# Loading the first output's weights: into the decoding's free places and into x's place after the last sums, instead of into x's place piece by piece

## The chip, the cores and the metric

One program on one core of a Trainium2 chip. The metric is the device time of one execution in microseconds (us); lower is better. Times of the kernel before come from three timed executions and from one profiled execution.

## The reference

```python
kv  = einsum('bhsd,bhse->bhde', k, v)            # 4 batches, 8 heads, 576 tokens, 64 wide
out = einsum('bhsd,bhde->bhse', q, kv)
x   = out / sqrt(mean(out*out) + 1e-6) * g_norm  # as 2304 tokens x 512
y   = ((x @ w_a) * (x @ w_b)) @ w_out            # 512 -> 1536 -> 512, the "first output" is y
h   = y @ w_in                                   # 512 -> 1024
s   = h * softmax(h); ln = layernorm(s) * g_ln
res = ln @ w_out2                                # 1024 -> 512
```

Everything is float32; the weights arrive as 64-bit floats.

## The kernel before, in words

**Arithmetic.** A float32 operand is kept as two parts, hi and lo, and each product is three matmuls on TensorE: hi*hi, lo*hi and hi*lo (lines 1035 to 1037 for the sums, line 1390 for the first output). The 64-bit weights are decoded on ScalarE (ACT), VectorE (DVE) and GpSimd (POOL); weights that are used later are written to HBM in hi and lo (line 588) and read back when their place is free.

**Stages.** First attention makes x. Then come the two products x @ w_a and x @ w_b, called the sums here. The d_ff dimension has 12 slices f of 128 and they are done in pairs fp. The last pairs use a scheme of seven block products (P1 to P7) over three token groups t, of 768 tokens each; a block product is done for w_a and then for w_b, six matmuls each. The products a*b go to HBM (`gm`, line 1057). Then y is computed (line 1390): 5 blocks j of tokens (384, 384, 512, 512, 512), within a block the 12 slices f, for each f four output slices d of 128, three matmuls each. For each (j, f) a tile `gi` is read from `gm` (line 1336), split into `gh` and `gl` (ACT line 1363, DVE line 1364), and multiplied with `wo[f]`, the hi and lo of w_out's slice f (512 KB). Then follows the second layer.

**Where x and wo lie.** x takes 73,728 bytes of each partition from offset XB on, in three pieces of tokens: 0 to 383, 384 to 1919 and 1920 to 2303 (line 281). A piece holds four planes of hi and then four planes of lo, one plane for 128 of the 512 channels. In the middle piece a plane is 6144 bytes. The weights of the first output reuse x's place (lines 309 to 316): wo[0] to wo[2] take the first piece, wo[3] to wo[8] the first 4096 bytes (tokens 384 to 1407) of six planes of the middle piece, wo[9] part of the last piece, and wo[10] and wo[11], in two halves of 256 KB each, the last 2048 bytes (tokens 1408 to 1919) of the first four planes of the middle piece.

**What sets the order.** The program's order on every engine is written out by a planner (`Order`) that keeps its own estimate of the time. All loads are issued by SyncE (SP), in order, on one queue. `c_loads` (line 1327) issues the loads of `gi` and of `wo`. A `wo[f]` is loaded when it is in HBM, when the planner's DMA backlog is under 3 us, and when in the last pair the token groups whose x lies in its place are done: t = 0 for f 0 to 2, t = 0 and 1 for f 3 to 8, all three for f 9 to 11. `c_item` (line 1371) holds the matmuls of one (j, f); its `ready` waits for the split `gi` and for `wo[f]`. Up to the last block products, items of the first output are put between them where `b_items` has fewer than three left. The semaphores between engines are set by the framework from the tiles that instructions read and write.

**The end of the sums in the last pair.** Token group 2 (tokens 1536 to 2303) runs last, in the order P1, P5, P2, P6, P3, P7, P4. P2 multiplies the raw x: for tokens 1536 to 1919, planes 2 and 3 of hi and lo in the middle piece. P5, P6 and P7 read sums kept elsewhere (`th`, `tl`), P3 and P4 the last piece. When no block product is left, the decoding of w_in opens (line 1767), and SP loads `raw` tiles of 512 KB for it (line 404).

**Free places.** The decoding uses WS (8192 bytes: two `f` tiles and the `ws` tiles) and STG (two staging tiles of 4096 bytes) until the last of w_out is in HBM. After that STG and WS are next written as the second half of w_in's sums (`bo`, line 323).

Of the kernel before, what the change touches and what calls it, by code (L numbers as in the profile page):

```python
# [9 lines left out]
F32 = mybir.dt.float32  # L10
F32R = mybir.dt.float32r
# [6 lines left out]
P = 128  # L18
# [5 lines left out]
NF1 = DF1 // P  # L24
# [13 lines left out]
CH = 512  # L38
# [167 lines left out]
def attention_moe_moe_kernel(ctx: ExitStack, tc, kv_in, kv_tail, q_in, g_norm, w1, w_in, w_out2, g_ln, out):  # L206
# [3 lines left out]
    nc = tc.nc  # L210
    INF = float("inf")
    M = Map(nc)
# [5 lines left out]
    od = Order()  # L218
# [9 lines left out]
    def ps_ready():  # L228
        return min(place_time(i) for i in range(4))
# [4 lines left out]
    def ps_tile(want=None):  # L234
        i = min(range(4), key=lambda i: (place_time(i) > od.now, want is not None and (i in wide) != want, place_time(i)))
        assert place_time(i) < INF
        bank[2 * i] = bank[2 * i + 1] = INF
        return i, PS[:, 2 * i:2 * i + 2]

    def ps_done(i):  # L240
        def done(t):
            bank[2 * i] = bank[2 * i + 1] = t

        return (None, 0, done)
# [61 lines left out]
    s_t = [M(f"s{i}", [P, 2, TB], F32, (M.R2 + 36864, M.R2 + 39936, M.AB + 4096)[i]) for i in range(3)]  # L306


    WO_AT = [4096 * f for f in range(3)] + [12288 + 6144 * k for k in range(6)] + [69632, (16384, 22528), (28672, 34816)]
    wo = []  # L310
    for f, at in enumerate(WO_AT):
        if isinstance(at, tuple):
            wo.append([M(f"wo{f}{n}", [P, CH], F32R, M.XB + a) for n, a in enumerate(at)])
        else:
            w = M(f"wo{f}", [P, 2, CH], F32R, M.XB + at)
            wo.append([w[:, 0], w[:, 1], w])
    gi_t = [M(f"gi{i}", [P, CH], F32, (M.T0 + 12288 if i < 3 else M.R2 + 6144) + 2048 * i) for i in range(6)]
    gs_t = [[M(f"g{x}{i}", [P, CH], F32R, M.R2 + 4096 * i + 2048 * n) for n, x in enumerate("hl")] for i in range(3)]
    ya = [M("ya0", [P, NP, HALVES[0]], F32, M.XB + 49152), M("ya1", [P, NP, HALVES[1]], F32, M.R2 + 18432)]
# [16 lines left out]
    def half(tok):  # L336
        return (0, tok) if tok < HALVES[0] else (1, tok - HALVES[0])
# [6 lines left out]
    for fp in range(PLAIN // 2, NF1 // 2):  # L344
        chunks += [("w", f, m) for m in range(2) for f in (2 * fp, 2 * fp + 1)]
        n = max(0, min(len(late_w), (0, 0, 0, 0, 0, 12)[fp]))
# [82 lines left out]
    w_ready, w_at, w_in_hbm, w_hbm = {}, {}, {}, {}  # L429
# [892 lines left out]
    c_units = [(j, f) for j in range(NBLK) for f in range(NF1)]  # L1322
    c_load = list(c_units)
    g_ready, wo_at = {}, {}
    y_ready = {}

    def c_loads():
        left = [steps_left.get((NF1 // 2 - 1, t)) for t in range(NTB // 2)]
        while left[:2] == [0, 0] and c_load and GI.ok():
            j, f = c_load[0]  # L1330
            t0, nb = BLOCKS[j]
            if max(g_at.get((f, i), INF) for i in range(t0 // P, (t0 + nb) // P)) > od.now:
                break
            c_load.pop(0)
            s = GI.take()
            nc.sync.dma_start(out=gi_t[s][:, 0:nb], in_=g_hbm[f][:, t0:t0 + nb])

            at = od.load(4 * nb * P)
            c_wait.append((j, f, s, nb, at))
            od.chain([(None, 0, c_split)], rank=0.5, t=at)  # L1340
        for f in range(NF1):
            if (f not in wo_at and not any(n != 0 for n in left[:1 + (f > 2) + (f > 8)]) and w_in_hbm.get(("wo", f), INF) <= od.now
                    and od.dma < od.now + 3):
                for n, o in enumerate(wo[f][2:] or wo[f]):
                    nc.sync.dma_start(out=o.bitcast(F32), in_=w_hbm["wo", f] if wo[f][2:] else w_hbm["wo", f][:, n])
                wo_at[f] = od.load(8 * CH * P)

    c_wait = []

# [21 lines left out]
    def c_item(j, f):  # L1371
        t0, nb = BLOCKS[j]
        hf, c0 = half(t0)

        def ready(d):
            t = max(g_ready.get((j, f), (INF,))[0], wo_at.get(f, INF))
            if f == 0 and d % 2 == 0:
                t = max(t, ps_ready())
            return t

        def run(d):
            if f == 0 and d % 2 == 0:
                c_ps[j, d // 2] = ps_tile()
            slot, ps = c_ps[j, d // 2]
            _, gh, gl, sg = g_ready[j, f]
            s = slice(d * P, (d + 1) * P)
            o = ps[:, d % 2, 0:nb]
            wh, wl = wo[f][0][:, s], wo[f][1][:, s]
            for n, (x, y) in enumerate(((wh, gh), (wh, gl), (wl, gh))):
                nc.tensor.matmul(o, lhsT=x, rhs=y, start=f == 0 and n == 0, stop=f == NF1 - 1 and n == 2)  # L1390
            if d == 3:
                GS.give(sg)
                od.chain([(None, 0, c_split)], rank=0.5, t=od.now)
            if f == NF1 - 1 and d % 2:
                dst = ya[hf][:, d - 1:d + 1, c0:c0 + nb]
                src = ps[:, :, 0:nb]

                def ready_(t):
                    if d == 3:
                        y_ready[j] = t  # L1400
                        a_more()

                od.chain([("A", 0.1 + 0.95 * nb / CH, lambda: nc.scalar.copy(out=dst, in_=src)), ps_done(slot), (None, 0, ready_)],
                         t=od.now + COST[nb] + 0.2)

        return [(COST[nb], lambda d=d: ready(d), lambda d=d: run(d)) for d in range(NP)]

    c_items = [x for j, f in c_units for x in c_item(j, f)]


# [12 lines left out]
    def a_more():  # L1423

        def has_y(i):
            return max(y_ready.get(j, INF) for j, (t0, nb) in enumerate(BLOCKS) if t0 < (i + 1) * 2 * P and t0 + nb > i * 2 * P)

        while todo_a and R_AO.ok() and ao_open(R_AO.taken % 2) and has_y(todo_a[0]) < INF:
            i = todo_a.pop(0)
            make_a(i, R_AO.take(), has_y(i))  # L1430
# [324 lines left out]
    def tick():  # L1755
        od.until(od.now)
        loads()
        decode_more()
        if not att_left[0] and 6 not in bank:
            bank[6] = bank[7] = od.now  # L1760
            for m in range(2):
                slot_free[m, 1] = od.now
        w_fill()
        a_more()
        x_sums()
        c_loads()
        if not b_items and not opened["i"]:
            opened["i"] = True
            F.cut(2)
            decode_more()  # L1770
# [4 lines left out]
    while any(ab) or busy or b_items or c_items:  # L1775
# [24 lines left out]
        if not plain and not att_left[0] and b_items:  # L1800
            n = next((n for n, x in enumerate(b_items[0:LOOK]) if x[1]() <= od.now), None)
# [108 lines left out]
```

## Time and profile before

| | |
|---|---|
| three timed executions | 674.08, 675.6 and 676.68 us, median 675.6 |
| the profiled execution | 675.45 us |
| its span, first to last instruction | 673.6 us |
| mean granted TensorE clock | 0.99 |
| TensorE busy | 649.2 us, 96% |

The profiled execution takes 1.85 us more than its span; that lies around the instructions. In rows of instructions the columns are start, length (both us), engine, line, operation, output<-inputs, shapes and count; a matmul's length overlaps with the next one's, so the pace is read from the starts. In brackets stands how long the engine was idle before, and what released it.

### The profile page before, as it was taken

Reading aid. Unit: us, or ns where it says so; the run is one execution under the profiler, and the core shown is the slowest. Engines: PE = TensorE matmul, PEld = TensorE weight load, DVE = VectorE, ACT = ScalarE, POOL = GpSimd, SP = SyncE. Lnnn points to the kernel's source line nnn. Section 1 sums busy time; section 2 is a strip of 40 time slices with the busy share of each in tenths; the row PEclk is TensorE's granted clock in tenths of the full one; section 3 lists DMA queues with packets and bytes.
Section 4 is the critical chain, followed back from the end, with each engine's and each line's share of the span. In section 5 each row is a group of like instructions: output and inputs, shape, how many; then the busy total and the mean of one; then the engine's idle time right before and its main releaser. Section 6 shows DMA issues by size and latency. Waiting matters only on the chain.

```text
span 673.6 us, 11084 instructions
## 1 busy us (share of the span) xinstructions
PE 649.2 (96%) x3994; PEld 579.7 (86%) x3994; DVE 491.7 (73%) x778; ACT 321.4 (48%) x538; POOL 214.3 (32%) x234
## 2 busy tenths in 40 slices
PE   5899999999999999997799999999999999999998
PEld 4778898899999999996799988888888888888887
DVE  2996889988998888862148878786369996687630
ACT  3777544444435434432034444453466765554431
POOL 1667101433111201001012424121488874552100
PEclk9999999999999999999699999999999999999999
DMA  8984698785699798895596554685604465433451
GB/s 331 376 292 155 221 299 295 261 283 200 252 367 352 281 406 311 318 339 190 173 306 205 182 160 133 202 271 185 226 28 129 139 207 167 133 111 101 140 173 47
DMA packets 93367, 150.68 MB, mean 224 GB/s; under 512 B 9472, under 2 KB 58880, under 8 KB 93312
## 3 DMA queue, kind: packets, MB, share of 16 engines
q1 hardware_dynamic: 93312, 149.98, 64.7%
q8 instruction: 31, 0.51, 0.3%
q14 instruction: 24, 0.20, 0.1%
HBM read 93.33 MB, written 56.62 MB: 223 GB/s over the span
## 4 chain that ended last, share of the span: by engine, by line
PE 80%; DMA 9%; DVE 5%; issue 2%; ACT 2%; SPq 1%; POOL 1%; ACTq 0%; DVEq 0%; POOLq 0%
PE ps L1390 22%; PE ps L1035 14%; PE ps L1036 14%; PE ps L1037 14%; PE ps L1532 13%; DMA kv<-in_kv 2%; DMA raw<-in_w 2%; DMA hb<-stg 2%; DMA wo<-hb_wo 1%; DVE ps L1156 1%; PE ps L876 1%; PE ps L919 1%; DMA yb<-sx 1%; DVE stg L646 1%; DMA wt<-hb 1%
## 5 line engine op out<-in xcount | busy, mean ns | idle before, releaser
L1390 PE MATMUL ps<-gh,wo 128*128 128x512 f32 (+1 forms) x480 | 137.7, 367 | 0.0
L1035 PE MATMUL ps<-xh,wt 128*128 128x384 f32 (+1 forms) x352 | 125.7, 357 | 9.9 <-DMA wo<-hb_wo 8.7
L1036 PE MATMUL ps<-xl,wt 128*128 128x384 f32 (+1 forms) x352 | 123.9, 352 | 0.0
L1037 PE MATMUL ps<-xh,wt 128*128 128x384 f32 (+1 forms) x352 | 123.9, 352 | 0.0
L1390 PEld LDWEIGHTS ps<-gh,wo 128*128 128x128 f32 x480 | 88.7, 188 | 11.3
L1390 PE MATMUL ps<-gl,wo 128*128 128x512 f32 (+1 forms) x240 | 88.1, 367 | 0.0
L1532 PE MATMUL ps<-bo,ao 128*128 128x512 f32 x378 | 87.2, 389 | 0.0
L1532 PEld LDWEIGHTS ps<-bo,ao 128*128 128x128 f32 x378 | 70.9, 188 | 14.7
L1035 PEld LDWEIGHTS ps<-xh,wt 128*128 128x128 f32 x352 | 66.6, 189 | 16.4 <-issue 5.2
L1364 DVE TENSOR_TENSOR gl<-gi,gh 128x512 fp32r<-128x512 f32 (+1 forms) x60 | 49.6, 829 | 39.6 <-ACT gh L1363 39.1
L1363 ACT CAST gh<-gi 128x512 fp32r<-128x512 f32 (+1 forms) x60 | 34.6, 579 | 79.6 <-PE ps L1390 68.2
L1036 PEld LDWEIGHTS ps<-xl,wt 128*128 128x128 f32 x352 | 66.7, 189 | 3.7
L1037 PEld LDWEIGHTS ps<-xh,wt 128*128 128x128 f32 x352 | 66.6, 189 | 3.8
L1036 PE MATMUL ps<-gw,dh 128*128 128x512 f32 (+1 forms) x152 | 57.4, 378 | 0.0
L1037 PE MATMUL ps<-gw,dl 128*128 128x512 f32 (+1 forms) x152 | 57.4, 378 | 0.0
L1035 PE MATMUL ps<-gw,dh 128*128 128x512 f32 (+1 forms) x152 | 57.4, 378 | 0.0
L1390 PEld LDWEIGHTS ps<-gl,wo 128*128 128x128 f32 x240 | 45.1, 188 | 5.5
L1035 PE MATMUL ps<-th,wt 128*128 128x384 f32 x144 | 48.9, 339 | 0.0
L1036 PE MATMUL ps<-tl,wt 128*128 128x384 f32 x144 | 48.7, 338 | 0.0
L1037 PE MATMUL ps<-th,wt 128*128 128x384 f32 x144 | 48.6, 337 | 0.0
L1284 ACT COPY s<-ps 128x768 f32<-128x768 f32 x24 | 19.3, 803 | 51.3 <-PE ps L1037 41.9
L615 POOL TENSOR_TENSOR f<-f,u 128x512 f32<-128x512 f32 x11 | 14.6, 1324 | 87.5 <-DVE u L480 87.5
(137 smaller groups left out, 1217.1 us busy)
## 6 DMA issues: line engine op xcount, KB each, us to landing
raw<-in_w SPq DMA_DIRECT2D x36, 512.0 KB, 6.4
hb<-stg SPq DMA_DIRECT2D x28, 512.0 KB, 5.5
wt<-hb SPq DMA_DIRECT2D x28, 512.0 KB, 6.5
gi<-gm SPq DMA_DIRECT2D x36, 256.0 KB, 2.7
su<-ya SPq DMA_DIRECT2D x34, 256.0 KB, 2.5
kv<-in_kv SPq DMA_DIRECT2D x16, 512.0 KB, 7.7
ya<-su SPq DMA_DIRECT2D x32, 256.0 KB, 3.0
hb_wo<-stg SPq DMA_DIRECT2D x12, 512.0 KB, 5.8
```

The costliest lines, as they stand in the source:

```text
L615: od.chain([("X", (0.62, 1.32), lambda e: tt(e)(out=f, in0=f, in1=u_t[su], op=ALU.add)), (None, 0, have)], rank=rank_of(k), t=t)
L646: lambda e: tt(e)(out=lo, in0=src, in1=hi.bitcast(F32), op=ALU.subtract))]
L876: nc.tensor.matmul(at(p)[h * D:(h + 1) * D], lhsT=k, rhs=v, start=c == 0 and p - pairs[0] < 2, stop=False, skip_group_check=True)
L919: nc.tensor.matmul(ps[m * w:(m + 1) * w, h, p * D:(p + 1) * D], lhsT=src[hs, m * w:(m + 1) * w], rhs=bds[b % 2][hs, p], start=True, stop=True)
L1035: nc.tensor.matmul(o, lhsT=ah, rhs=bh, start=first, stop=False, skip_group_check=skip)
L1036: nc.tensor.matmul(o, lhsT=ah, rhs=bl, start=False, stop=False, skip_group_check=skip)
L1037: nc.tensor.matmul(o, lhsT=al, rhs=bh, start=False, stop=last, skip_group_check=skip)
L1284: return [("A", 2 * AC - 0.1, lambda: nc.scalar.copy(out=s_t[i], in_=pair_of(at))), is_(what)]
L1363: ("A", 0.08 + 0.5 * k, lambda g=g, gh=gh: nc.scalar.copy(out=gh, in_=g)),
L1364: ("S", 0.08 + 0.54 * k, lambda g=g, gh=gh, gl=gl: nc.vector.tensor_tensor(out=gl, in0=g, in1=gh.bitcast(F32), op=ALU.subtract)),
L1390: nc.tensor.matmul(o, lhsT=x, rhs=y, start=f == 0 and n == 0, stop=f == NF1 - 1 and n == 2)
L1532: nc.tensor.matmul(o, lhsT=x, rhs=y, start=first and k == m == 0, stop=k == 1 and m == 2, skip_group_check=not first)
```

## The change

All twelve `wo[f]` get consecutive places of 4096 bytes in x's place. For f 3 to 6 there is a second tile, `wo_first[f]`, in WS and STG, used for block 0 alone. The loads form a fixed list: wo 0 to 2 when t = 0 is done; then `wo_first` 3 to 6 when all of w_out is in HBM; then wo 7 to 11 when all three token groups are done; then wo 3 to 6 for the blocks after the first. The limit of 3 us on the planner's DMA backlog stays. All loads are of 512 KB: 16 instead of 10 and 4 halves.

```diff
-    WO_AT = [4096 * f for f in range(3)] + [12288 + 6144 * k for k in range(6)] + [69632, (16384, 22528), (28672, 34816)]
-    wo = []
-    for f, at in enumerate(WO_AT):
-        if isinstance(at, tuple):
-            wo.append([M(f"wo{f}{n}", [P, CH], F32R, M.XB + a) for n, a in enumerate(at)])
-        else:
-            w = M(f"wo{f}", [P, 2, CH], F32R, M.XB + at)
-            wo.append([w[:, 0], w[:, 1], w])
+    wo = [M(f"wo{f}", [P, 2, CH], F32R, M.XB + 4096 * f) for f in range(NF1)]
+    wo_first = {f: M(f"wof{f}", [P, 2, CH], F32R, at) for f, at in zip(range(3, 7), (M.WS, M.WS + 4096, M.STG, M.STG + 4096))}
...
+    wo_load = [(f, f in wo_first) for f in range(NF1)] + [(f, False) for f in wo_first]
...
-        for f in range(NF1):
-            if (f not in wo_at and not any(n != 0 for n in left[:1 + (f > 2) + (f > 8)]) and w_in_hbm.get(("wo", f), INF) <= od.now
-                    and od.dma < od.now + 3):
-                for n, o in enumerate(wo[f][2:] or wo[f]):
-                    nc.sync.dma_start(out=o.bitcast(F32), in_=w_hbm["wo", f] if wo[f][2:] else w_hbm["wo", f][:, n])
-                wo_at[f] = od.load(8 * CH * P)
+        while wo_load and od.dma < od.now + 3:
+            f, first = wo_load[0]
+            if first:
+                ok = max(w_in_hbm.get(("wo", x), INF) for x in range(NF1)) <= od.now
+            else:
+                ok = not any(n != 0 for n in left[:3 if f > 2 else 1]) and w_in_hbm.get(("wo", f), INF) <= od.now
+            if not ok:
+                break
+            wo_load.pop(0)
+            nc.sync.dma_start(out=(wo_first if first else wo)[f].bitcast(F32), in_=w_hbm["wo", f])
+            wo_at[f, first] = od.load(8 * CH * P)
...
+        first = j == 0 and f in wo_first
+        w = (wo_first if first else wo)[f]
 
         def ready(d):
-            t = max(g_ready.get((j, f), (INF,))[0], wo_at.get(f, INF))
+            t = max(g_ready.get((j, f), (INF,))[0], wo_at.get((f, first), INF))
...
-            wh, wl = wo[f][0][:, s], wo[f][1][:, s]
+            wh, wl = w[:, 0, s], w[:, 1, s]
```

## Rows read from the trace of the kernel before

**Rows 1.** The page: busy tenths of TensorE and its granted clock, 40 slices.
```profile
PE   5899999999999999997799999999999999999998
...
PEclk9999999999999999999699999999999999999999
```
**Rows 2.** Waits of TensorE, 290 to 345 us (us in total, times, longest).
```profile
PE ps L1035 <- DMA wo<-hb_wo: 8.7, 2, 4.9
```
**Rows 3.** Timeline of TensorE, last block products of token group 2.
```profile
314.80 0.34 PE L1037 MATMUL ps<-th,wt 128*128 128x384 f32 x1
320.07 0.66 PE L1035 MATMUL ps<-xh,wt 128*128 128x384 f32 x1 [4.94 <-DMA wo<-hb_wo]
...
326.08 0.69 PE L1035 MATMUL ps<-xh,wt 128*128 128x384 f32 x1 [3.74 <-DMA wo<-hb_wo]
...
330.72 0.40 PE L1037 MATMUL ps<-th,wt 128*128 128x384 f32 x1
...
331.48 0.35 PE L1035 MATMUL ps<-xh,wt 128*128 128x384 f32 x1
...
333.58 0.33 PE L1035 MATMUL ps<-th,wt 128*128 128x384 f32 x1
...
335.49 0.33 PE L1037 MATMUL ps<-th,wt 128*128 128x384 f32 x1
...
337.22 0.33 PE L1035 MATMUL ps<-xh,wt 128*128 128x384 f32 x1
...
339.13 0.33 PE L1037 MATMUL ps<-xh,wt 128*128 128x384 f32 x1
```
**Rows 4.** Timeline of SP: issues of wo and their neighbours.
```profile
297.55 0.32 SPq L588 DMA_DIRECT2D hb_wo<-stg  x1
297.96 1.15 SPq L1345 DMA_DIRECT2D wo<-hb_wo  x2
...
299.71 0.42 SPq L1345 DMA_DIRECT2D wo<-hb_wo  x1
...
311.42 2.78 SPq L1336 DMA_DIRECT2D gi<-gm  x6
314.60 0.32 SPq L1345 DMA_DIRECT2D wo<-hb_wo  x1
...
322.36 0.32 SPq L1345 DMA_DIRECT2D wo<-hb_wo  x1
...
329.93 1.35 SPq L1345 DMA_DIRECT2D wo<-hb_wo  x3
```
**Rows 5.** Stretches: busy us and count by engine, then clock, DMA share, GB/s.
```profile
300.00:305.00 5.00, 5.00 (x31) 5.00 (x30) 0.56 (x1) 1.47 (x3) 0.00 (x0) 1.00 0.99 363
305.00:310.00 5.00, 5.00 (x31) 5.00 (x30) 1.92 (x2) 0.61 (x1) 1.04 (x2) 1.00 0.10 36
310.00:315.00 5.00, 5.00 (x30) 4.82 (x28) 0.56 (x1) 1.26 (x2) 0.98 (x1) 1.00 0.65 196
315.00:320.00 5.00, 0.14 (x1) 0.00 (x0) 1.50 (x3) 2.03 (x4) 0.00 (x0) 0.72 0.77 253
320.00:325.00 5.00, 2.26 (x6) 1.78 (x6) 0.00 (x0) 0.48 (x1) 0.00 (x0) 0.50 0.35 87
```
**Rows 6.** Timeline of ACT and DVE: the copies on which P7 and P4 wait.
```profile
331.81 0.80 ACT L1284 COPY s<-ps 128x768 f32<-128x768 f32 x1 [8.96 <-PE ps L1037]
...
335.86 0.96 DVE L1299 TENSOR_TENSOR s<-ps,s 128x768 f32<-128x768 f32 x1 [1.07 <-PE ps L1037]
```
**Rows 7.** DMA issue at 322.36 us: count, size, us to landing.
```profile
wo<-hb_wo SPq DMA_DIRECT2D x1, 512.0 KB, 3.7
```
**Rows 8.** Stretches as in rows 5, after the last block product.
```profile
340.00:345.00 5.00, 5.00 (x30) 5.00 (x30) 1.81 (x4) 1.92 (x4) 0.00 (x0) 1.00 0.95 319
345.00:350.00 5.00, 5.00 (x31) 5.00 (x30) 3.44 (x8) 2.17 (x4) 0.00 (x0) 1.00 0.97 328
...
345.00:360.00 15.00, 15.00 (x89) 15.00 (x88) 12.11 (x20) 6.40 (x12) 4.06 (x3) 1.00 0.88 295
360.00:375.00 15.00, 15.00 (x88) 15.00 (x87) 12.82 (x21) 7.77 (x14) 5.35 (x5) 1.00 0.57 172
...
645.00:660.00 15.00, 15.00 (x68) 12.43 (x67) 3.50 (x3) 3.39 (x5) 0.00 (x0) 1.00 0.49 152
```
**Rows 9.** Writes of w_in's sums over their whole stage: lengths, first and last start.
```profile
L736 ACT CAST bo<-bt x14: 613/616/623, 352.9 to 423.8; 128x512 fp32r<-128x512 f32 x14
```

## The prediction

> **What bounds the kernel now.** I read the page first. TensorE is busy in nearly every slice, and its granted clock is full except around one place, in the middle of the span, where both rows dip [rows 1]. So the time is TensorE's work plus that dip. The waits of TensorE in that stretch name one releaser: the loads of wo, two waits, 8.7 us [rows 2]. The timeline shows them in front of the two halves of P2 of token group 2 [rows 3]: TensorE stops after 314.80, waits 4.94 us, does six matmuls, waits 3.74 us, does six more. SP's timeline gives the partner of each wait: wo[3] is issued at 314.60 and wo[4] at 322.36, each just ahead of one half of P2 [rows 4].
>
> P2 needs neither weight. It reads tokens 1536 to 1919 of planes 2 and 3, and wo[3] and wo[4] are written over tokens 384 to 1407 of planes 0 and 1: no byte in common. What they share is the middle piece of x as one tile. I infer that the semaphores guard that tile as a whole: P2's first half waits until wo[3] has landed, wo[4] may only be written after that half has read, and P2's second half waits for wo[4]. Two things speak for it. wo[0] to wo[2], which go into the first piece, are issued between 297.96 and 300.1 [rows 4], and TensorE is busy for all of 300 to 315 [rows 5]. And the next loads, from 329.93 on, come when only `th`, `tl` and the last piece are left to read; no wait follows. The clock adds to the price: in 315 to 320 TensorE works 0.14 us and the granted clock averages 0.72; in 320 to 325 it is 0.50, which is the 1.2 GHz level [rows 5].
>
> **What the change takes away.** From the matmul at 314.80 to the last one of P4 at 339.13 are 24.33 us and 69 matmul starts: 60 of P2, P6, P3, P7 and P4, and nine of the first output. At the full clock 23 steps take from 331.48 to 335.49, 0.1743 us each; at the lower clock 14 steps take from 326.08 to 330.72, 0.331 each [rows 3]. At full pace the 69 would need 12.03 us, so the dip costs 24.33 - 12.03 = **12.3 us**: 8.7 of waiting, 3.6 of slow matmuls. In the changed kernel nothing is loaded into the middle piece until P4 has been issued, so both waits lose their cause. TensorE then has no gap, and no reason to fall to the lower clock.
>
> What is late next? P7 needs a copy of P6 by ACT: before, that copy begins 331.81 and ends 332.61, 0.97 us ahead of P7's first matmul at 333.58. P4 needs the addition on DVE that ends 336.82; nine matmuls of the first output cover it, and P4 begins right behind them at 337.22 [rows 3, 6]. Both stand at the full clock in the old trace, so the same cover holds; without the nine matmuls P4 would wait about 1 us.
>
> **What it adds.** *Four early loads* (wo_first), 4 x 0.524 MB = 2.1 MB. The last store of w_out is issued at 297.55 [rows 4], so they come from about 302 on, behind wo[0] to wo[2]. At the 363 GB/s of 300 to 305 they take 5.8 us, and the queue is nearly empty then: DMA share 0.10 in 305 to 310 [rows 5]. At worst they push the six gi loads at 311.42 back by 5.8 us. The first of these is used nine matmuls before P4, near 323.5, so this costs nothing. The tiles in WS and STG are read by f 3 to 6, near 332 to 340; w_in's sums begin to be written at 352.9, or 12 us earlier once P4 is earlier, and the first half of them goes elsewhere [rows 9]. Nothing.
>
> *Loads after P4.* wo[3] to wo[8] used to be loaded while TensorE waited or worked on the sums; now wo 7 to 11 and again 3 to 6, nine loads or 4.7 MB, follow P4, together with the raw tiles of w_in. P4 ends at T = 314.80 + 12.03 + 0.33 = 327.2. The rest of f 0 takes 0.5 us and each f 12 x 0.1743 = 2.09 us, so f 7 starts at T + 13.1, f 11 at T + 21.4, f 3 of block 1 at T + 29.8. With the planner's order as I work it out from the backlog limit, ahead of and including wo[11] stand five wo loads, four raw tiles (0.524 MB each), six gi and two products (192 KB, 0.197 MB each): 6.3 MB. A 512 KB load alone lands after 3.7 us [rows 7], of which 1.4 are its bytes at 363 GB/s, so the fixed part is 2.3, and I count 2.4. At 335 GB/s, between the 328 of the fullest stretch with this mixture and the 363 with wo loads alone [rows 5, 8], wo[11] lands at T + 18.8 + 2.4 = T + 21.2, just in time. At 295 GB/s, the mean of 345 to 360 [rows 8], it lands at T + 23.8, 2.4 us late. wo[10] and everything before it are earlier by more than a load. The second wo[3] to wo[6] have 4 us or more of margin. I take 0, because 319 and 328 are measured where the queue is full and 295 contains time when it is not, and keep 0 and 2.4 as the ends.
>
> Queued loads of 512 KB reach 363 GB/s at a DMA share of 0.99 [rows 5]. The Trainium skill, page "DMA: Bandwidth & Descriptors", section "Bandwidth", speaks against loads of this size: it asks for transfers of 1 MiB or more to get three quarters of the peak, about 327 GB/s. By that wo[11] would be 0.3 us late and the gain 12.0 us; by the row it is 12.3, and I keep the row.
>
> *Fewer parts.* Two halves become one load, twice; SP spends about 0.4 us less per pair, and it is not the bound: nothing.
>
> **Sum.** From 345 us to 660 TensorE is busy without a gap [rows 8], so what P4 gains arrives at the end. The profiled execution took 675.45, which is 0.15 under the median of 675.6. 675.45 - 12.3 = 663.15; against the median **663.3 us**.
>
> **Rivals.** *Loads after P4 come late.* For it: the queue is full already at 340 to 350 [rows 8], and after P4 now come nine wo loads instead of three loads' worth, 3.1 MB more. Against: the backlog limit holds the loads behind the gi tiles, and their deadlines lie 2 us apart. At 295 GB/s it costs 2.4 us, 665.7; at 250, 6.3/0.25 + 2.4 = 27.6, 6.2 us late, 669.5.
>
> *Slower than before.* The same queue, where it delivers far less: wo[11] landing 12.3 us after T + 21.4 undoes the gain, 6.3 MB in 31.3 us or 201 GB/s. At the 172 GB/s of 360 to 375 [rows 8] it would be 17.6 us late: 680.9. Against: that stretch has a DMA share of 0.57, so it asked for no more; from a full queue the rows show no rate near it.
>
> *The waits stay.* If TensorE is held by something other than the shared tile, the same two stops return in front of P2: 675.5. Against: only loads into the middle piece have a wait behind them.
>
> **How the numbers follow.** Forecast 0.70, late loads 0.20, waits stay 0.06, slower 0.04. A measurement here can tell about 0.5%, 3.4 us, from no change. Forecast and late loads both lie below 672.2: faster 0.90, same 0.06, slower 0.04. The range begins 1.5 us under the forecast, which is how far the fastest execution lies under the median, at 661.8, and ends at 667.5, where late loads have cost 4.2 us; that leaves out the two last rivals and the tail of late loads.
>
> **What would show it.** Right: no wait of TensorE on wo ahead of P2, the clock at 1.00 from 300 to 340, P4's last matmul near 327, four wo loads between 302 and 311, and TensorE without a gap from there to the end. Wrong: gaps in front of line 1390's first matmul of f 7 to 11, or in block 1 at f 3 to 6, released by the loads of wo (late loads); the two gaps ahead of P2 again (waits stay); an end of line 1390 that is less than 12 us earlier although P4 is (given back later).

## The result, and the profile after

The changed kernel takes 664.23 us, median of 5 executions (663.02 to 665.27), beside 675.6 us of the kernel before (5 executions, 674.08 to 676.94). The ratio is 0.9832 with a 95% interval of 0.981 to 0.9855: 11.4 us less, where 12.3 was forecast, inside the stated range of 661.8 to 667.5.

The profiled execution after took 665.05 us, span 663.3, mean granted clock 0.997. The code above line 1390 has moved by six lines or fewer: lines 1035 to 1037 are now 1029 to 1031, 1336 is 1331, 404 is 398; line 1390 is now 1392.

First the page: busy tenths of TensorE and its granted clock, in 40 slices.

```profile
PE   4889998999999999999999999999999999999998
...
PEclk9899999999999999999999999999999999999999
```

The dip in the middle [rows 1] is gone from both rows. What is left below 9 lies in the first quarter and, for TensorE's work, in the last slice. The waits of TensorE between 300 us and the end are an empty list; the two waits of [rows 2] have no successor. The timeline of TensorE, from the last matmul of P5 over the first of P2 to the last of P4, answers to [rows 3]:

```profile
316.63 0.33 PE L1031 MATMUL ps<-th,wt 128*128 128x384 f32 x1
316.81 0.33 PE L1029 MATMUL ps<-xh,wt 128*128 128x384 f32 x1
...
328.60 0.33 PE L1031 MATMUL ps<-xh,wt 128*128 128x384 f32 x1
```

P2 starts 0.18 us behind the start of the matmul before it, at full pace. The stretch takes 328.60 - 316.63 = 11.97 us; it took 24.33. That is 12.36 us, and the 69 matmuls were reckoned at 12.03.

The stretches show where the loads went; columns as in [rows 5], the last three are the clock, the DMA share and GB/s.

```profile
305.00:310.00 5.00, 5.00 (x31) 5.00 (x30) 1.10 (x2) 0.80 (x1) 0.22 (x1) 1.00 1.04 417
...
315.00:320.00 5.00, 5.00 (x31) 5.00 (x30) 2.29 (x5) 2.52 (x5) 0.00 (x0) 1.00 0.84 262
...
330.00:345.00 15.00, 15.00 (x88) 15.00 (x87) 9.39 (x18) 5.66 (x12) 1.59 (x1) 1.00 1.03 391
```

Two things are to be seen. The stretch of 305 to 310, nearly empty in [rows 5] at a share of 0.10, now carries the early loads, of which three are issued there. And the 15 us behind P4 run the queue full, at 391 GB/s, while TensorE stays busy for every microsecond of them at the full clock.

### The profile page after: what moved, and what is told of

Its sections match the earlier page's. It is cut to its first block, busy times and chain, and to the rows that moved or that the text cites. A ratio compares the mean times of both kernels' runs of the same rounds, so it can differ in the third digit from the quotient of the medians.

```text
span 663.3 us, 11087 instructions
## 1 busy us (share of the span) xinstructions
PE 643.4 (97%) x3994; PEld 576.1 (87%) x3994; DVE 492.5 (74%) x778; ACT 321.1 (48%) x538; POOL 215.9 (33%) x234
## 4 chain that ended last, share of the span: by engine, by line
PE 87%; DMA 7%; DVE 2%; ACT 2%; issue 1%; SPq 1%; ACTq 0%; DVEq 0%
PE ps L1392 22%; PE ps L1029 17%; PE ps L1030 16%; PE ps L1031 16%; PE ps L1534 13%; DMA wt<-hb 2%; DMA raw<-in_w 1%; PE ps L913 1%; DMA kv<-in_kv 1%; DMA q<-in_q 1%; PE ps L870 1%; DMA gm<-g 1%; DMA yb<-sx 1%; PE ps L1002 1%; DVE g L1086 0%
## 5 line engine op out<-in xcount | busy, mean ns | idle before, releaser
L1392 PE MATMUL ps<-gh,wo 128*128 128x512 f32 (+1 forms) x448 | 129.8, 369 | 0.0
L1392 PEld LDWEIGHTS ps<-gh,wo 128*128 128x128 f32 x448 | 83.0, 188 | 11.2
L1392 PE MATMUL ps<-gl,wo 128*128 128x512 f32 (+1 forms) x224 | 82.8, 369 | 0.0
L1364 DVE TENSOR_TENSOR gl<-gi,gh 128x512 fp32r<-128x512 f32 (+1 forms) x60 | 48.0, 805 | 36.8 <-ACT gh L1363 36.4
L1392 PEld LDWEIGHTS ps<-gl,wo 128*128 128x128 f32 x224 | 42.0, 188 | 5.6
L453 ACT ACTIVATE u<-raw 128x512 f32<-128x512 f32 x52 | 34.8, 670 | 15.2 <-DMA raw<-in_w 13.3
```

The costliest lines, as they stand in the source:

```text
L453: nc.scalar.activation(out=u, in_=w[:, :, 1].bitcast(F32), func=AF.Abs)
L1364: ("S", 0.08 + 0.54 * k, lambda g=g, gh=gh, gl=gl: nc.vector.tensor_tensor(out=gl, in0=g, in1=gh.bitcast(F32), op=ALU.subtract)),
```

## The experiments

Every experiment was timed in 6 or 12 executions beside the kernel before, which had a median of 676.41 in the first four (23 executions) and 675.24 in the last two (11). In brackets stand the lowest and the highest execution, and for a ratio its 95% interval.

**One load moved back (e3).** The changed kernel, but the second wo[3], which nobody uses before block 1, goes into the middle piece ahead of P2, over bytes that P2 does not read.

```diff
-    wo_load = [(f, f in wo_first) for f in range(NF1)] + [(f, False) for f in wo_first]
+    wo_load = [(f, f in wo_first) for f in range(7)] + [(3, False)] + [(f, False) for f in (7, 8, 9, 10, 11, 4, 5, 6)]
...
-                ok = not any(n != 0 for n in left[:3 if f > 2 else 1]) and w_in_hbm.get(("wo", f), INF) <= od.now
+                ok = not any(n != 0 for n in left[:2 if f == 3 else 3 if f > 2 else 1]) and w_in_hbm.get(("wo", f), INF) <= od.now
```

> The changed kernel with one load moved back: the second wo[3], which is not used before block 1, is loaded into x's middle piece when token groups 0 and 1 are done, ahead of P2; its bytes are tokens 384 to 1407 of a plane that P2 does not read. If the guard is the piece as a whole, TensorE waits once, 4 to 5 us, ahead of P2, and works at the lower clock for some microseconds behind it, 2 to 4 us more: 670 to 673. If bytes or the need for the weight decide, no wait: 664.

Measured: 672.28 us (669.33 to 673.54), ratio 0.9938 (0.9916 to 0.996). The load in its timeline of SP:

```profile
313.23 0.38 SPq L1345 DMA_DIRECT2D wo<-hb_wo  x1
```

And its timeline of TensorE, from the last matmul of P5 over the first of P2 to the last of P4:

```profile
313.48 0.34 PE L1031 MATMUL ps<-th,wt 128*128 128x384 f32 x1
319.25 0.66 PE L1029 MATMUL ps<-xh,wt 128*128 128x384 f32 x1 [5.43 <-DMA wo<-hb_wo]
...
332.95 0.33 PE L1031 MATMUL ps<-xh,wt 128*128 128x384 f32 x1
```

The wait is back in its old place, once, in front of a P2 that needs neither the weight nor those bytes. From P5 to P4 it takes 19.47 us, 7.5 more than the changed kernel: 5.43 of waiting and 2.07 of slow matmuls. Need and bytes are out; what P2 shares with the load is the tile. By the code that tile is half of what the prediction called one: `xp` (line 281) makes the hi planes of a piece one tile and its lo planes another. wo[3] and wo[4] lie in the hi tile, which P2 reads from its first matmul on; no run tells the hi tile from the whole piece.

**The tile cut (e2, with its control e2c).** The kernel before, with x cut at token 1536 so that token group 2 has tiles of its own; wo[f] then lies at 4096 f, and all loads from wo[3] on may start when token groups 0 and 1 are done, as early as wo[3] did before. No block may cross the cut, so the pairs without block products go in six blocks of 384. The control has the six blocks alone.

```diff
-XBLOCKS = [FIVE] * 4
+XBLOCKS = [SIX] * 4
...
-        return [x for js in ((4, 3), (2, 1), (0,)) for i in range(2) for j in js for x in of(i, j)]
+        return [x for js in ((5, 4), (3, 2), (1, 0)) for i in range(2) for j in js for x in of(i, j)]
```

That is the control. The cut adds to it:

```diff
-    XP = [0, 384, 1920, NT]
+    XP = [0, 384, 1536, 1920, NT]
...
-        i = sum(t0 >= x for x in XP[1:3])
+        i = sum(t0 >= x for x in XP[1:4])
...
-    WO_AT = [4096 * f for f in range(3)] + [12288 + 6144 * k for k in range(6)] + [69632, (16384, 22528), (28672, 34816)]
+    WO_AT = [4096 * f for f in range(NF1)]
...
-            if (f not in wo_at and not any(n != 0 for n in left[:1 + (f > 2) + (f > 8)]) and w_in_hbm.get(("wo", f), INF) <= od.now
+            if (f not in wo_at and not any(n != 0 for n in left[:1 + (f > 2)]) and w_in_hbm.get(("wo", f), INF) <= od.now
```

> Control for the split: the kernel before with six blocks of 384 tokens for the pairs without block products, x in three pieces and wo's places as before. From 0.1743 us for 384 columns and 0.2267 for 512, six blocks cost 1.0458 instead of 1.0287 us per plane, 96 times: 1.6 us more, 677.2, with the two waits ahead of P2 still there.

> The kernel before, with x in four pieces instead of three, cut at token 1536, so that token group 2 shares no piece with the places of wo (wo[f] at 4096 f, all loaded after token groups 0 and 1, as early as before); the pairs without block products go in six blocks of 384 tokens, as no block may cross the cut. To be held against e2c. If the guard is the piece as a whole, the loads of wo are issued ahead of P2 as before and TensorE does not wait: 12 us less than e2c, about 665. If TensorE was held by the loads in another way (their bytes, the queue, their number), the two waits stay: 677.

Measured: the control 676.98 us, ratio 1.002 (0.9997 to 1.0044); the cut 665.19 us, ratio 0.9844 (0.9814 to 0.9875). The waits of TensorE between 300 and 345 us in the control are one row; in the cut kernel the list is empty, although its SP issues wo[3] just ahead of P2 and wo[4] while P2 runs. The row of the control, then of the cut kernel SP's issues and the first matmul of P2:

```profile
PE ps L1035 <- DMA wo<-hb_wo: 9.0, 2, 5.3
```

```profile
316.22 0.38 SPq L1345 DMA_DIRECT2D wo<-hb_wo  x1
...
317.12 0.43 SPq L1345 DMA_DIRECT2D wo<-hb_wo  x1
```

```profile
316.61 0.33 PE L1035 MATMUL ps<-xh,wt 128*128 128x384 f32 x1
```

P2 starts 0.18 us behind the start of P5's last matmul, and from P5 to P4 it takes 11.96 us, where the control takes 23.98. The medians differ by 11.8 us. wo[3] comes 0.21 us before P5's last matmul in the cut kernel and 0.12 before it in the control, so it was not moved behind P2. So it was not the loads as such, nor their traffic beside P2, that held TensorE: it was the tile. With the experiment before, this settles the cause from both sides. The six blocks cost 0.6 us by the medians, where 1.6 was reckoned; the interval holds both.

**The gate alone (e1).** The kernel before, where all loads from wo[3] on wait for the last sums; no early places.

```diff
-            if (f not in wo_at and not any(n != 0 for n in left[:1 + (f > 2) + (f > 8)]) and w_in_hbm.get(("wo", f), INF) <= od.now
+            if (f not in wo_at and not any(n != 0 for n in left[:3 if f > 2 else 1]) and w_in_hbm.get(("wo", f), INF) <= od.now
```

> The kernel before with one edit: wo 3 to 11 are loaded only when all three token groups are done; no early places in WS and STG. If the guard of x's middle piece is the cause, both waits ahead of P2 are gone and P4 ends 12 us earlier. If the early places are needed to cover the loads after P4, then wo[5] or a later one is late: each f takes 2.1 us on TensorE and each load with its gi tile about 2 us of the queue, behind three raw tiles of 1.5 us each, so I expect 2 to 5 us of waiting in block 0 and a time of 666 to 670. If the early places do nothing, 664 as the changed kernel. If the whole gain came from the early places and not from the gate, 675.

Measured: 668.51 us (665.99 to 670.14), ratio 0.9893 (0.9859 to 0.9928). From P5 to P4 it takes 11.96 us, as in the changed kernel. Then the first output waits, by the count of its matmuls for wo[5], wo[8] and wo[9]. The timeline of TensorE after P4, its waits and the matmul ahead of the first:

```profile
336.22 0.34 PE L1390 MATMUL ps<-gh,wo 128*128 128x384 f32 x1
339.18 0.41 PE L1390 MATMUL ps<-gh,wo 128*128 128x384 f32 x1 [2.62 <-DMA wo<-hb_wo]
...
346.90 0.41 PE L1390 MATMUL ps<-gh,wo 128*128 128x384 f32 x1 [1.23 <-DMA wo<-hb_wo]
...
349.41 0.41 PE L1390 MATMUL ps<-gh,wo 128*128 128x384 f32 x1 [0.16 <-DMA wo<-hb_wo]
```

4.0 us in three waits, with the queue full: 407 GB/s in its 335 to 340. The part behind P4 is 4.8 us longer than in the changed kernel (339.5 to 334.7). Nearly all of the other 0.8 lies at the same three places: from 336.22 over 339.18 to the next matmul at 339.43 two steps take 3.21 us, where 0.35 is the full pace, so the stop costs 2.86 us and not 2.62: the idle time in brackets counts from the end of a matmul that the next one would have overlapped. The other two stops cost 0.24 more than their idle time as well (345.33 to 347.15 and 348.91 to 349.66), 4.7 us in all, at a granted clock of 1.00. So the change has two parts. The gate takes the waits away, and the early places, with the order of loads that goes with them, cover the start of block 0 while the queue is behind. This is the rival "late loads" as it looks when its cover is missing.

**The wait filled with work (e5).** The kernel with one load moved back, but the last six matmuls of P5 are done six times over, each time from the start of the sum, so the value stays the same.

```diff
-            for k in range(2):
+            for k in list(range(2)) * (6 if (fp, t, name, m) == (NF1 // 2 - 1, 2, "P5", 1) else 1):
                 sl = slice(c * 256 + k * P, c * 256 + (k + 1) * P)
```

> The kernel e3, with the last six matmuls of P5 of token group 2 done six times over (each time from the start of the sum, so the value stays), 30 more matmuls or 5.2 us, where e3 waits 5.4 us for the load. It tells the clock from the wait. If the slow matmuls behind the wait come from TensorE having been idle, they are gone: the granted clock stays at 1.00, and from the last matmul of P5 (of the first time over) to the last of P4 it takes 17.4 us instead of e3's 19.47, about 2 us less in the time than e3. If they come from something else in that stretch, such as the traffic, it is as e3.

Measured: 669.53 us (665.41 to 672.93), ratio 0.9902 (0.9866 to 0.9939). The stretches around the wait, first of the kernel that waits idle, then of the one that fills the wait:

```profile
315.00:320.00 5.00, 0.75 (x2) 0.78 (x3) 1.50 (x3) 0.89 (x3) 0.00 (x0) 0.64 0.77 266
320.00:325.00 5.00, 5.00 (x22) 5.00 (x22) 0.56 (x1) 0.48 (x1) 0.00 (x0) 0.68 0.04 13
```

```profile
315.00:320.00 5.00, 4.67 (x27) 4.38 (x27) 1.99 (x4) 2.42 (x5) 0.00 (x0) 1.00 0.28 97
320.00:325.00 5.00, 5.00 (x31) 5.00 (x30) 1.01 (x2) 0.80 (x1) 0.30 (x1) 1.00 0.45 151
```

With 30 useless matmuls the granted clock stays at 1.00 and only 0.3 us of waiting is left. The stretch to P4 takes 12.56 us from the last of the 30, so 12.56 + 30 x 0.1743 = 17.8 from the first time over, 1.7 less than the 19.47 with an idle wait; 17.4 was expected. The medians are 2.8 us apart, but the intervals of the two ratios overlap, so it is the stage that decides, not the time. The slow matmuls are the price of idling, not of the traffic: in 320 to 325 the DMA share was 0.04 where TensorE had idled and 0.45 where it had not.

**The changed kernel again.**

> The changed kernel once more, beside the same runs of the kernel before as e5. The prediction's 12.3 us stood in one stage; the medians differ by 11.4. If the 0.9 us is the spread of the part ahead of that stage from execution to execution, the stage from the last matmul of P5 to the last of P4 takes 12.0 us again, the part behind it 334.5 to 334.7, and only the part ahead differs; the ratio stays within 0.981 to 0.9855. If the change costs 0.9 us behind P4, the part behind is near 335.4.

Measured: 664.01 us (661.51 to 665.76), ratio 0.9817 (0.9785 to 0.985). In its profiled execution the stretch from P5 to P4 takes 11.96 us again, and the part behind it 334.71 (334.70 in the first profile, 334.47 before the change). The part ahead differs: the last matmul of P5 starts at 314.80 before the change, at 316.63 and 316.83 in the two profiles of the changed kernel, and, counting from the first time over, at 313.48 and 316.39 - 5.23 = 311.2 in the two kernels made from it, whose program up to there is the same. It varies by over 5 us from execution to execution. The median of the ratio was forecast at 663.3/675.6 = 0.9818, inside both intervals.

## Why the prediction was right

*The cause and its price.* Two waits and slow matmuls, 12.3 us in one stage: measured 12.36 and 12.37 in the two profiles of the changed kernel, against the one of the kernel before. The inference that the guard is on the piece of x as a whole rested on two signs in the old trace; it is now shown, by a load that brings the wait back without any need and by a cut that removes it with a load still issued ahead of P2. Only the size of the tile is told too large, as said above.

*The split into waiting and clock.* 8.7 and 3.6 us were read from the old rows. Filling the wait shows that the second part belongs to idling. Not all of it is the clock: read from the starts, a stop in the gate alone costs 0.24 us more than its idle time while the granted clock is 1.00.

*What would be late next.* P7 and P4 followed without a gap, as the same cover held. Nothing else took the place of the wait.

*The loads after P4.* The right answer, nothing, from a term that was sized wrong, and so in part by luck: the prediction set 6.3 MB at 335 GB/s and had wo[11] land at T + 21.2, just in time, and both of its errors made the load earlier. SP issued it earlier than I had worked out, and the queue was faster. The issue, and its time to landing:

```profile
339.31 0.42 SPq L1345 DMA_DIRECT2D wo<-hb_wo  x1
```

```profile
wo<-hb_wo SPq DMA_DIRECT2D x1, 512.0 KB, 5.6
```

T is 328.60 + 0.33 = 328.93, so it is issued at T + 10.4, ahead of the fourth raw tile instead of behind it, and lands after 5.6 us, at T + 16.0. By the prediction's count f 11 needs it at T + 21.4: 5.4 us to spare instead of 0.2. The rate behind P4 was 391 GB/s. The 319 and 328 GB/s of [rows 8], which I took for a full queue, came at shares of 0.95 and 0.97 and are not the most that the queue gives. The old trace said so already, in stretches that the prediction did not use. One of them, with loads and stores:

```profile
240.00:255.00 15.00, 15.00 (x88) 15.00 (x87) 13.15 (x24) 6.79 (x12) 1.29 (x1) 1.00 1.03 412
```

A share near 1 alone does not tell the rate: the kernel with the gate alone moved 340 GB/s at a share of 1.00 in its 300 to 305. What held the rate down in such stretches stays open.

The Trainium skill, page "DMA: Bandwidth & Descriptors", section "Bandwidth", asks for transfers of 1 MiB or more to reach three quarters of the peak; with the 436 GB/s that it gives as the peak, that is 327 GB/s by estimate. Its table is of loads issued from GpSimd. The trace differs: 512 KB loads and smaller tiles, issued by SyncE in one queue, moved 391 GB/s over 15 us. The Trainium skill, page "HBM Reference", section "Specifications (TRN2)", says that a core that streams alone reaches about 425 GB/s. The 417 of 305 to 310, with one core at work, agrees.

*The early loads.* TensorE has no wait from 300 us on in either profile of the changed kernel, so they cost nothing there, as reckoned, and the gate alone shows what they are worth: 4.0 us of waiting that is not there, and 4.3 us between the medians.

*The total.* 0.9 us of the 12.3 is missing in the first median and 1.1 in the second. It does not lie in the stage, and behind it at most 0.25 us do (334.47 before, 334.70 and 334.71 after). The part ahead of the stage varies by more than what is missing: in the profiled execution after it was 1.83 us longer than in the one before, so P4's last matmul stood at 328.60 where 327 was forecast, and these two executions differ by 10.4 us alone. The intervals of the ratio hold the forecast, and the runs can't tell whether the change takes anything ahead of the stage.

## What to carry to other kernels

When a tile is reused piece by piece, look at which object the semaphores guard: a load over bytes that nobody needs any more can still stop the reader of its neighbour, and the trace shows it as a wait of an engine on data that it does not use. Cut the tile where its parts die at different times, or load after the last reader and find other places for what is needed first. Price an idle wait of TensorE with the matmuls behind it: here 2 to 4 us on top of 5 to 9 where the granted clock fell, and 0.7 on top of 4.0 in the gate alone, where it stayed at 1.00. And read a queue's rate from the fullest stretches of the whole trace, not only from those near the place.

## What was not expected of the hardware

The queue gave much more than the 335 GB/s that the prediction counted on: 391 GB/s over 15 us behind P4 and up to 417 in a stretch of 5 us; the old trace had it too, 412 GB/s from 240 to 255. And useless matmuls in place of an idle wait were worth 1.7 us from P5 to P4, with the granted clock at 1.00 instead of 0.64 and 0.68.
